# Wider packets for the second weight, renumbered columns of the first layer, and a new order of steps in an RWKV-and-MLP kernel

## The chip, the cores and the metric

The kernel runs on one core of one Trainium2 chip. The metric is the device time of one execution in microseconds (us). A core has five engines that work side by side: TensorE (PE, with its weight loads shown apart as PEld), VectorE (DVE), ScalarE (ACT), GpSimd (POOL) and SyncE (SP). DMAs are issued from SP, ACT and POOL and are moved by sixteen shared DMA engines.

## The reference

Two stages follow each other. The first is a linear attention with decay, for 4 batches, 8 heads, 768 positions and heads of 48:

```python
for t in range(S):
    cur = np.einsum('bhd,bhe->bhde', u[None] * kt, vt)
    y[:, :, t] = np.einsum('bhd,bhde->bhe', rt, state + cur)
    state = w[None, :, :, None] * state + np.einsum('bhd,bhe->bhde', kt, vt)
```

The second is a two-layer network over the 3072 rows of 384 numbers that come out of it, with 2048 columns in the middle:

```python
h = x @ w_in                                   # 384 -> 2048
g = np.where(h >= 1, h, np.where(h <= -1, 0.0, (h + 1) ** 2 / 4))
out = g @ w_out                                # 2048 -> 384
```

## The kernel before

The sequence is cut into twelve groups, g = 0 to 11, of 256 rows each. Groups 0 to 3 are "paired" (256 positions of one batch, two neighbours in a partition); the others hold 128 positions of two batches. Group 0 alone is worked in two halves of its heads for many steps; their names then end in .0 and .1.

Everything is written as named steps, and the string ORDER lists them all: each engine does its steps in the order of that list, in order, and waits where its data isn't there. `@D`, `@A` and `@P` put a step on DVE, ACT or POOL, and `#0` to `#3` name the pair of PSUM banks that the step takes. A pair can be taken again when the tile that held it has been read for the last time. There is no scheduler beside that list.

The steps of one group g, with their engine where it is fixed:

- `ldR`, `ldK`, `ldV` load r, k and v from SP's queue, one load of 384 KB each (half of that for the halves of group 0). Loads of one kind share three buffers (V's are called V32).
- `Rs`, `Ks` multiply r and k with tables of powers of w (W2 for paired groups, made at the start from w by `wB`, `ln`, `wu`, `wd`) into the bf16 tile RK. `Vc` casts v to bf16 (tile Vb).
- `KU` = k times r, `RU` = KU times u, `us` (DVE) = the sum of RU over a head, `ud` = Vb times that sum: the term of the current position, tile V2 or V2b. `uB` and `uc` spread u over all partitions (u_bc).
- `T` (PE) transposes RK, `TT` copies the result to RKT. From group 4 on `RK` does both by a DMA transpose on SP's queue.
- `A` (PE) makes the scores, `AT` (DVE) masks them.
- `Sp` (PE) makes a chunk's part of the state, `Ta`, `Tm` (DVE) and `dc` decay and add it, `sa` and `sb` make bf16 copies for PE.
- `Y` (PE) sums the output of the attention, `y` copies it, adding V2 for unpaired groups. `X` (PE) and `xT` transpose it; from group 4 on `xT` is a DMA transpose on SP's queue.
- `up` g.q (PE) is a quarter of the first layer: 512 of the 2048 columns in four blocks f of 128, 12 matmuls of 256 columns with w_in as the weight that is loaded (line 543). `re` and `sq` (ACT, lines 550 and 554) and `ga` (DVE, line 558) apply the activation.
- `dn` g.j.q (PE) is a quarter of the second layer for 128 of the rows: four matmuls of 384 columns with w_out (line 565). `o` copies the sum (line 123), `st` stores it.

The weights come from POOL's queue, cast to bf16 on the way, each in two halves: `wi` 0 and 1 (line 288) for quarters 0-1 and 2-3 of w_in, `wo` 0 and 1 (line 292) for w_out. Block n of w_out is rows 128 n to 128 n + 127, one row in each partition:

```python
w_out_src = moe_w_out.rearrange("(no ni) d -> ni no d", ni=P)
```

so one partition's share of a block is one piece of 384 numbers, 768 bytes as bf16. `kw` n (line 300) are n matmuls on a tile of zeros whose result nobody reads; they keep PE going in the gaps of the start, in a bank pair that each `kw` names.

Of the kernel before, what the change touches and what calls it, by code (L numbers as in the profile page):

```python
# [9 lines left out]
F32 = mybir.dt.float32  # L10
# [5 lines left out]
P = 128  # L16
# [11 lines left out]
W_IN_ENDS, W_OUT_ENDS = [2, 4], [2, 4]  # L28
# [42 lines left out]


# [1 line left out]
def kernel(  # L74
# [11 lines left out]
    nc = tc.nc  # L86
    B, H, S, D = r.shape
# [4 lines left out]
    nK = DM // P  # L92
    nF = DF // P
    BP = B // 2
    NCH = S // C
    FG = 4
    NQ = nF // FG
# [16 lines left out]
    def bank(slot, what, key, shape, dtype):  # L114
        t = psum.tile(shape, dtype, name=what, tag=f"s{slot}")
        live[(what,) + key] = t
        return t

    def got(what, *key):
        return live[(what,) + key]  # L120
# [8 lines left out]
    w_in_sb = const.tile([P, nK, DF], BF16, name="w_in_sb")  # L129
    w_out_sb = const.tile([P, nF, DO], BF16, name="w_out_sb")  # L130
    w_in_src = moe_w_in.rearrange("(ko ki) n -> ki ko n", ki=P)
    w_out_src = moe_w_out.rearrange("(no ni) d -> ni no d", ni=P)
    mark = const.tile([1, 16], BF16, name="mark")
    w_row = const.tile([1, DM], F32, name="w_row")
    u_row = const.tile([1, DM], F32, name="u_row")
# [152 lines left out]
        nc.gpsimd.dma_start(out=w_in_sb[:, :, n], in_=w_in_src[:, :, n])  # L288

    def step_wo(e, s, i):  # L290
        n = slice(([0] + W_OUT_ENDS)[i] * nF // NQ, W_OUT_ENDS[i] * nF // NQ)
        nc.gpsimd.dma_start(out=w_out_sb[:, n, :], in_=w_out_src[:, n, :])

    def step_mk(e, s, i):
        nc.sync.dma_start(out=mark, in_=w_in_sb[:1, 0, :16])

    def step_kw(e, s, n):
        t = bank(s, "idle", (), [P, 4 * P], F32)
        for _ in range(n):
            nc.tensor.matmul(t, warm[:, :P], warm, start=True, stop=True, skip_group_check=True)  # L300

# [236 lines left out]
    def step_up(e, s, g, q):  # L538
        hp = bank(s, "hp", (g, q), [P, FG, 2 * P], F32)
        for f in range(FG):  # L540
            n0 = (q * FG + f) * P
            for i in range(nK):
                nc.tensor.matmul(  # L543
                    hp[:, f].rearrange("p (j t) -> p j t", j=2), w_in_sb[:, i, n0 : n0 + P], got("xT", g)[:, :, i, :], start=(i == 0), stop=(i == nK - 1),
                    skip_group_check=True,
                )

# [76 lines left out]
```

## Time and profile before

| | |
|---|---|
| three runs, median (lowest to highest) | 179.48 us (179.13 to 179.93) |
| the profiled execution | 179.18 us |
| its span on the core | 177.4 us |
| granted clock of TensorE | 1.00 |
| PE, DVE, ACT, POOL busy | 94%, 72%, 71%, 64% of the span |
| moved by DMA | 28.09 MB, mean 158 GB/s |

The span goes from the first to the last instruction of the program. A row of the order in time gives the start, the length, the engine, the line and the operation, what it writes and reads with the shape, how many were merged (x), and in square brackets how long the engine stood idle before it and what ended that. A row of the waits gives who waited for whom: the total in us, how often, the longest. A row of a DMA queue gives packets, MB and the time of the packets as a share of sixteen engines' time; q1 is SP's queue, q0 POOL's. Durations of PE's matmuls overlap, so the distance from one block to the next is the better measure of what a matmul costs.

### The profile page before, as it was taken

How to read it: one execution, taken by the hardware profiler on the slowest of the kernel's cores; microseconds unless marked ns; L12 is line 12 of the kernel's file. 1: busy time of each engine (PE TensorE's matmuls, PEld its weight loads, DVE VectorE, ACT ScalarE, POOL GpSimd, SP SyncE). 2: the span in 40 equal slices, each digit the busy share in tenths (PEclk: the TensorE clock that was granted, in tenths of full speed). 3: DMA queues.
4: the chain of work that ended last, by engine and by line, in shares of the span. 5: the costliest groups of instructions: out<-in, count | busy, mean ns of one | idle time of the engine just before them, and what ended most of it. 6: DMA issues, size and time to landing. Idle time of an engine off the chain costs nothing.

```text
span 177.4 us, 4658 instructions
## 1 busy us (share of the span) xinstructions
PE 167.6 (94%) x1976; PEld 119.0 (67%) x1979; DVE 127.7 (72%) x152; ACT 125.4 (71%) x151; POOL 113.8 (64%) x95
## 2 busy tenths in 40 slices
PE   7997998979999999999999999999999999899990
PEld 2544677646778678677687766777676875778750
DVE  5789766585577978998737789747879498682660
ACT  2854599866699949639769884489882891777931
POOL 6235959991799999981999453999854593500000
PEclk9999999999999999999999999999999999999999
DMA  6999999999989045919989949989959988140022
GB/s 141 266 256 211 234 221 218 190 221 215 181 209 230 15 93 97 176 40 217 237 134 233 202 82 220 178 159 231 148 143 131 148 188 134 26 137 0 0 89 89
DMA packets 91753, 28.09 MB, mean 158 GB/s; under 512 B 85842, under 2 KB 90964, under 8 KB 91732
## 3 DMA queue, kind: packets, MB, share of 16 engines
q1 hardware_dynamic: 88432, 24.65, 70.8%
q0 software_dynamic: 2880, 3.15, 10.3%
q8 instruction: 15, 0.25, 0.6%
q10 hardware_dynamic: 420, 0.00, 0.1%
q14 instruction: 6, 0.05, 0.1%
HBM read 20.45 MB, written 4.72 MB: 142 GB/s over the span
## 4 chain that ended last, share of the span: by engine, by line
PE 83%; DMA 7%; DVE 4%; ACT 1%; issue 1%; POOL 1%; ACTq 0%; DVEq 0%
PE op L565 35%; PE hp L543 30%; DMA w_out_sb<-in_moe_w_out_dram 7%; PE idle L300 3%; PE A L394 3%; PE Y L508 2%; PE A L388 2%; PE T L359 1%; PE Y L501 1%; PE Sp L426 1%; DVE RK L318 1%; PE Y L480 1%; PE Sp L419 1%; PE X L529 1%; DVE AT L406 1%
## 5 line engine op out<-in xcount | busy, mean ns | idle before, releaser
L558 DVE SCALAR_TENSOR_TENSOR gt<-sq,hp 128x1024 bf16<-128x1024 f32 x48 | 58.1, 1217 | 20.4 <-ACT sq L554 20.1
L565 PE MATMUL op<-w_out_sb,gt 128*128 128x384 bf16 x384 | 70.6, 326 | 2.0 <-DMA w_out_sb<-in_moe_w_out_dram 2.0
L543 PE MATMUL hp<-xT,w_in_sb 128*128 128x256 bf16 x576 | 69.0, 273 | 0.0
L550 ACT ACTIVATE pt<-hp 128x1024 f32<-128x1024 f32 x48 | 48.7, 1017 | 26.0 <-PE hp L543 25.6
L543 PEld LDWEIGHTS <-w_in_sb 128*128 128x128 bf16 x576 | 55.4, 98 | 9.6 <-issue 0.3
L554 ACT ACTIVATE sq<-pt 128x1024 f32<-128x1024 f32 x48 | 50.6, 1057 | 1.4
L565 PEld LDWEIGHTS <-gt 128*128 128x128 bf16 x384 | 35.6, 98 | 22.9 <-issue 1.3
L318 POOL TENSOR_TENSOR RK<-K,W 128x768 bf16<-128x768 f32 (+1 forms) x11 | 19.4, 1764 | 5.7 <-ACT W L267 3.6
L333 POOL TENSOR_TENSOR RU<-KU,u_bc 128x768 f32<-128x768 f32 x11 | 20.0, 1816 | 0.6
L326 POOL TENSOR_TENSOR KU<-K,R 128x768 f32<-128x768 f32 x11 | 20.0, 1820 | 0.0
L318 POOL TENSOR_TENSOR RK<-R,W 128x768 bf16<-128x768 f32 x10 | 18.2, 1825 | 2.5 <-DMA R<-in_r_dram 2.5
L406 DVE TENSOR_TENSOR AT<-A,mask 128x1024 bf16<-128x1024 f32 x16 | 19.1, 1216 | 0.6 <-PE A L394 0.5
L347 POOL TENSOR_TENSOR V<-Vb,us 128x768 f32<-128x768 bf16 x8 | 11.8, 1476 | 8.3 <-ACT Vb L123 5.1
L123 DVE COPY o<-op 128x384 f32<-128x384 f32 x10 | 5.3, 553 | 10.6 <-PE op L565 10.6
L123 ACT COPY o<-op 128x384 f32<-128x384 f32 x14 | 6.2, 479 | 8.0 <-PE op L565 7.9
L339 DVE TENSOR_REDUCE us<-RU 128x16 f32<-128x768 f32 (+1 forms) x13 | 11.4, 882 | 0.0
L460 POOL TENSOR_TENSOR state<-Tm,wCm 128x384 f32<-128x384 f32 (+1 forms) x9 | 7.8, 865 | 5.2 <-DVE Tm L454 4.8
L400 DVE TENSOR_TENSOR AT<-A,mask 128x1024 bf16<-128x1024 f32 x8 | 9.5, 1218 | 2.2 <-PE A L388 2.2
L347 POOL TENSOR_TENSOR V2b<-Vb,us 128x384 bf16<-128x384 bf16 (+1 forms) x4 | 4.6, 1150 | 9.7 <-ACT Vb L123 4.9
L300 PE MATMUL idle<-warm 128*128 128x512 bf16 x22 | 8.4, 493 | 1.6 <-DVE w_col L141 1.2
L523 DVE TENSOR_TENSOR y<-Y,V 128x768 bf16<-128x768 f32 x8 | 7.6, 954 | 0.9 <-POOL V L347 0.3
L123 ACT COPY RKT<-T 128x1024 bf16<-128x1024 bf16 x5 | 5.0, 1013 | 4.4 <-PE T L359 4.4
(85 smaller groups left out, 121.8 us busy)
## 6 DMA issues: line engine op xcount, KB each, us to landing
V<-in_v_dram SPq DMA_DIRECT2D x12, 384.0 KB, 4.8
R<-in_r_dram SPq DMA_DIRECT2D x11, 384.0 KB, 6.2
K<-in_k_dram SPq DMA_DIRECT2D x11, 384.0 KB, 5.7
out_dram<-o SPq DMA_DIRECT2D x7, 384.0 KB, 3.0
out_dram<-o SPq DMA_DIRECT2D x10, 192.0 KB, 3.1
w_in_sb<-in_moe_w_in_dram POOLq DMA_DIRECT2D x2, 768.0 KB, 11.2
w_out_sb<-in_moe_w_out_dram POOLq DMA_DIRECT2D x2, 768.0 KB, 11.0
K<-in_k_dram SPq DMA_DIRECT2D x2, 192.0 KB, 3.1
```

The costliest lines, as they stand in the source:

```text
L123: nc.scalar.copy(out, in_) if e == "A" else engines[e].tensor_copy(out, in_)
L300: nc.tensor.matmul(t, warm[:, :P], warm, start=True, stop=True, skip_group_check=True)
L318: engines[e].tensor_mul(RK[g % NB][:, x, :, hs, :D], rows(got(what, g), g)[:, :, hs], table(x, g, hs))
L326: engines[e].tensor_mul(got("KU", g)[:, :, hs], rows(got("K", g), g)[:, :, hs], rows(got("R", g), g)[:, :, hs])
L333: engines[e].tensor_mul(got("RU", g)[:, :, hs], got("KU", g)[:, :, hs], u_rep)
L347: engines[e].tensor_mul(got("V2", g)[:, :, hs], got("Vb", g)[:, :, hs], sums)
L406: nc.vector.tensor_mul(t.rearrange("p i n t -> p (i n) t"), got("A", g, h).rearrange("p i n t -> p (i n) t"), mask)
L543: nc.tensor.matmul(hp[:, f].rearrange("p (j t) -> p j t", j=2), w_in_sb[:, i, n0 : n0 + P], got("xT", g)[:, :, i, :], start=(i == 0), stop ...
L550: nc.scalar.activation(t, got("hp", g, q), AF.Relu, bias=0.5, scale=0.5)
L554: nc.scalar.activation(t, got("pt", g, q), AF.Square)
L558: nc.vector.scalar_tensor_tensor(out=t, in0=got("sq", g, q), scalar=1.0, in1=got("hp", g, q), op0=ALU.min, op1=ALU.max)
L565: nc.tensor.matmul(got("op", g)[:, j, :DO], got("gt", g, q)[:, f, j * P : (j + 1) * P], w_out_sb[:, n, :], start=(n == 0), stop=(n == nF - 1),
```

## The change

Four things change, and with them some line numbers by one.

The rows of w_out are dealt out anew: of the 512 rows of a quarter q, partition p takes the four neighbours 4p to 4p + 3. They lie side by side in memory, so a partition's share of a quarter is one piece of 4 x 384 numbers, 3072 bytes as bf16. For the second layer to meet the right rows, block f of the first layer's quarter must hold the columns 4p + f. The weight tile w_in stays as it is in memory; the matmul of `up` reads every fourth column of it, a step of 8 bytes.

The idle matmuls take one bank pair once (`kw5#0`) and later ones write to the same tile (`got("idle")`), where each block took a pair of its own before. There are 18 instead of 25.

All steps stand in a new order. Some change their engine: KU0.0, RU0.1, dc1, ud1, Vc7, Vc9 and sb4 go to POOL; KU1, TT1.0, TT3.0, uc, wu1.1, y3 and o1.0, o2.1, o3.1 to DVE; Vc5, Vc8, sa0, sb0, sb7, xT0, o2.0 and the o copies of groups 4, 6, 8 and 9 to ACT.

```diff
 ORDER = """
-wr@A ur@A kw6#0 wB0#0 ldK0.0 ldR0.0 ldR0.1 cl tb KU0.0@D ln0 wu0.0@A wu1.0@D wd1.0@A wd0.0@D Rs0.0@D Ks0.0@D ldK0.1
+wr@A ldK0.0 ur@A cl ldR0.0 ldK0.1 ldR0.1 tb kw5#0 wB0#1 ln0 wd1.0@A wd0.0@D wu0.0@A wu1.0@D Rs0.0@D wB1#2 ln1 wd1.1@A
...
-    w_out_src = moe_w_out.rearrange("(no ni) d -> ni no d", ni=P)
+    w_out_src = moe_w_out.rearrange("(q p f) d -> p q (f d)", p=P, f=FG)
...
     def step_wo(e, s, i):
-        n = slice(([0] + W_OUT_ENDS)[i] * nF // NQ, W_OUT_ENDS[i] * nF // NQ)
-        nc.gpsimd.dma_start(out=w_out_sb[:, n, :], in_=w_out_src[:, n, :])
+        q = slice(([0] + W_OUT_ENDS)[i], W_OUT_ENDS[i])
+        nc.gpsimd.dma_start(out=w_out_sb.rearrange("p (q f) d -> p q (f d)", f=FG)[:, q, :], in_=w_out_src[:, q, :])
...
     def step_kw(e, s, n):
-        t = bank(s, "idle", (), [P, 4 * P], F32)
+        t = got("idle") if s is None else bank(s, "idle", (), [P, 4 * P], F32)
...
     def step_up(e, s, g, q):
...
-            n0 = (q * FG + f) * P
             for i in range(nK):
                 nc.tensor.matmul(
-                    hp[:, f].rearrange("p (j t) -> p j t", j=2), w_in_sb[:, i, n0 : n0 + P], got("xT", g)[:, :, i, :], ...
+                    hp[:, f].rearrange("p (j t) -> p j t", j=2), w_in_sb.rearrange("p i (q n f) -> p i q f n", q=NQ, f=FG)[:, i, q, f], got("xT", g)[:, :, i, :], ...
```

75 lines of the change are left out of this document (37 added, 38 removed).

## Prediction

> **What bounds the kernel now.** I read the waits first, then the engines' busy time by stretch, then the order in time of the first 42 us on each engine.
>
> ```profile
> PE op L565 <- DMA w_out_sb<-in_moe_w_out_dram: 2.0, 2, 1.2
> PE Y L501 <- DVE AT L406: 0.5, 1, 0.5
> ...
> 41.00:61.00 20.00, 20.00 (x342) 14.91 (x335) 13.81 (x18) 16.94 (x25) 15.13 (x11) 1.00 0.92 178
> 121.00:141.00 20.00, 20.00 (x214) 14.48 (x213) 15.12 (x15) 14.78 (x17) 12.78 (x9) 1.00 0.94 164
> ```
>
> In the two rows by stretch the columns are the length, then the busy time of PE, PEld, DVE, ACT and POOL, the granted clock, the DMA share and GB/s. PE has no gap there: 20.00 of 20.00 at clock 1.00, and no other engine is near its limit. So between about 41 and 173 us only PE's own work counts, and it is the same matmuls in both kernels. Time can be won only where PE is not yet full, or does work that nobody needs: the start, the two waits for w_out, and the half microsecond at the last Y.
>
> ```profile
> 1.19 2.74 PE L300 MATMUL idle<-warm 128*128 128x512 bf16 x6 [1.19 <-DVE w_col L141]
> ...
> 10.79 0.62 PE L359 MATMUL T<-ident,RK 128*128 128x128 bf16 x8
> ...
> 19.49 0.50 PE L529 MATMUL X<-ident,y 128*128 128x128 bf16 x6
> ...
> 20.85 2.79 PE L543 MATMUL hp<-xT,w_in_sb 128*128 128x256 bf16 x24
> ...
> 26.48 4.09 PE L543 MATMUL hp<-xT,w_in_sb 128*128 128x256 bf16 x36
> 31.39 2.77 PE L565 MATMUL op<-w_out_sb,gt 128*128 128x384 bf16 x16 [0.82 <-DMA w_out_sb<-in_moe_w_out_dram]
> ...
> 37.08 1.46 PE L565 MATMUL op<-w_out_sb,gt 128*128 128x384 bf16 x8 [1.16 <-DMA w_out_sb<-in_moe_w_out_dram]
> ```
>
> The first row of the first layer (up0.0) starts at 20.85; from there to 30.57 PE is dense. It then stands 0.82 us for the first half of w_out, and 1.16 us for the second. What sets 20.85 is DVE, which works through this without a long gap:
>
> ```profile
> 6.50 0.55 DVE L318 TENSOR_TENSOR RK<-R,W 128x384 bf16<-128x384 f32 x1
> 6.97 0.55 DVE L318 TENSOR_TENSOR RK<-K,W 128x384 bf16<-128x384 f32 x1
> ...
> 9.19 0.68 DVE L123 COPY RKT<-T 128x1024 bf16<-128x1024 bf16 x1
> ...
> 11.83 0.95 DVE L318 TENSOR_TENSOR RK<-R,W 128x768 bf16<-128x768 f32 x1
> 12.69 0.95 DVE L318 TENSOR_TENSOR RK<-K,W 128x768 bf16<-128x768 f32 x1
> 13.56 1.02 DVE L333 TENSOR_TENSOR RU<-KU,u_bc 128x384 f32<-128x384 f32 x2
> 14.50 1.00 DVE L339 TENSOR_REDUCE us<-RU 128x8 f32<-128x384 f32 x2
> 15.42 0.35 DVE L436 TENSOR_TENSOR state<-Sp,wCm 128x192 f32<-128x192 f32 x1
> 15.80 0.36 DVE L451 TENSOR_TENSOR Tm<-Sp,state 128x192 f32<-128x192 f32 x1
> 16.07 3.48 DVE L400 TENSOR_TENSOR AT<-A,mask 128x1024 bf16<-128x1024 f32 x3
> ```
>
> **The start.** The first block of idle matmuls loses one of six, 2.74 / 6 = 0.46 us, so the broadcast of w and all behind it can begin 0.46 us earlier if the row of w has landed by 3.5 us; the trace does not show that landing, and if it is late this term is 0. On DVE I add up the new order from Rs0.0 (now at 6.50 - 0.46 = 6.04) to AT0.1, from start to start in the rows above: three operations of half a tile 3 x 0.47, wu1.1 0.35 (nearest row: 15.42), the copy u_bc 0.46 (below, on ACT), TT0.0 0.68, RU0.0 0.47, us0.0 0.46, Rs0.1 0.47, Rs1 0.86, Ta0 0.38, us0.1 0.46, AT0.0 1.16, Tm0 0.27, AT0.1 1.16. That is 8.6 us, so AT0.1 ends at 14.6. Before it ended at 16.07 + 1.16 = 17.2: the gain is that Ks1, one RU and one KU go behind it or to POOL. Waits: Rs1 is reached at 10.3, and it needs the load of R1.
>
> ```profile
> 3.44 0.80 SPq L227 DMA_DIRECT2D R<-in_r_dram  x1
> ...
> R<-in_r_dram SPq DMA_DIRECT2D x1, 384.0 KB, 5.7
> ...
> q1 hardware_dynamic: 4818, 1.81, 112.2%
> ...
> L123 ACT COPY u_bc<-uB 128x384 f32<-128x384 f32 x1 | 0.5, 455 | 0.0
> ...
> L123 ACT CAST y<-Y 128x768 bf16<-128x768 f32 x3 | 2.4, 789 | 0.4 <-PE Y L487 0.4
> ```
>
> R1 landed at 3.44 + 5.7 = 9.1. V1 now goes ahead of it on SP, and SP's queue moved 1.81 MB from 2 to 9 us, so 0.39 MB more is 1.5 us: R1 lands at 10.6, a wait of 0.3. I put AT0.1's end at 15.0.
>
> From there to up0.0 took 20.85 - 17.2 = 3.6 us. Now two branches run. One is Y0.1, y0.1, X0 (0.50) and xT0, which is a copy on ACT (0.8 by the y row): some 2.9 us with Y0.1's 0.7. The other decides, since PE takes A1.0 and T1.1 ahead of up0.0: Ks1 0.86, KU1 0.86, TT1.0 0.68 on DVE, then A1.0 (sixteen small matmuls, at most the 0.51 of the L508 row below) and T1.1 (0.62) on PE, 3.5 us. So up0.0 starts at 18.5, at 19.0 if w lands late: 2.4 or 1.9 earlier. A1.1, some 0.4 us, was ahead of up0.0 and is now behind it: **net 1.5 to 2.0, I take 1.8**. The six up blocks from there to the first dn0 are the same and took 9.7 us; ACT has the same work in that stretch, so I cost its new order at nothing.
>
> In these rows the names are tiles: RK the scaled r and k, KU and RU the products for the diagonal, AT the masked scores, W2 the tables. DVE before, from the first RK:
>
> ```order
> L318 TENSOR_TENSOR RK_78<-R_148,W2_133 128x2x4x48
> L318 TENSOR_TENSOR RK_78<-K_146,W2_134 128x2x4x48
> L326 TENSOR_TENSOR KU_154<-K_146,R_148 128x2x192
> L318 TENSOR_TENSOR RK_78<-R_148,W2_133 128x2x4x48
> L123 COPY RKT_189<-T_180 128x1024
> L400 TENSOR_TENSOR AT_213<-A_196,mask2_109 128x1024
> L318 TENSOR_TENSOR RK_79<-R_218,W2_133 128x16x48
> L318 TENSOR_TENSOR RK_79<-K_220,W2_134 128x16x48
> L333 TENSOR_TENSOR RU_294<-KU_154,u_bc_71 128x2x192 x2
> ```
>
> And DVE now, from the copy of the first transposes to the second AT:
>
> ```order
> L122 COPY RKT_189<-T_180 128x1024
> L334 TENSOR_TENSOR RU_191<-KU_166,u_bc_71 128x2x192
> L340 TENSOR_REDUCE us_194<-RU_191 128x2x4
> L319 TENSOR_TENSOR RK_78<-R_141,W2_133 128x2x4x48
> L319 TENSOR_TENSOR RK_79<-R_202,W2_133 128x16x48
> L437 TENSOR_TENSOR state_122<-Sp_206,wCm_84 128x192
> L340 TENSOR_REDUCE us_194<-RU_191 128x2x4
> L401 TENSOR_TENSOR AT_262<-A_245,mask2_109 128x1024
> L452 TENSOR_TENSOR Tm_329<-Sp_206,state_122 128x192
> L401 TENSOR_TENSOR AT_335<-A_286,mask2_109 128x1024
> ```
>
> The full RK from K_220 (Ks1) no longer stands between the two AT, and one of the two RU is gone from DVE.
>
> **The weight loads.** POOL issues them, and each row here gives start and length of the issue; the rows of landings are of w_in, then of w_out.
>
> ```profile
> 8.79 1.71 POOL L288 DMA_DIRECT2D w_in_sb<-in_moe_w_in_dram  x2
> ...
> 19.48 1.81 POOL L333 TENSOR_TENSOR RU<-KU,u_bc 128x768 f32<-128x768 f32 x1
> 21.24 0.94 POOL L292 DMA_DIRECT2D w_out_sb<-in_moe_w_out_dram  x1
> ...
> 25.23 0.94 POOL L292 DMA_DIRECT2D w_out_sb<-in_moe_w_out_dram  x1
> ...
> DMA to landing us min/median/max: 9.7/11.2/12.7
> ...
> DMA to landing us min/median/max: 10.1/11.0/11.8
> ...
> q0 software_dynamic: 269, 0.52, 91.3%
> q1 hardware_dynamic: 268, 0.10, 19.4%
> ...
> q0 software_dynamic: 381, 0.29, 92.9%
> q1 hardware_dynamic: 383, 0.08, 34.2%
> ...
> q1 hardware_dynamic: 1778, 0.35, 123.7%
> ```
>
> POOL before, from its first scaled k to the first half of w_out (state and sd are the running state, V2b the diagonal term):
>
> ```order
> L318 TENSOR_TENSOR RK_78<-K_146,W2_134 128x2x4x48
> L288 DMA w_in_sb_66<-in_moe_w_in_dram 128x3x1024 x2
> L347 TENSOR_TENSOR V2b_301<-Vb_224,us_298 128x2x192
> L123 CAST sd_126<-state_122 48x4x48 x2
> L347 TENSOR_TENSOR V2b_301<-Vb_224,us_298 128x2x192
> L326 TENSOR_TENSOR KU_402<-K_220,R_218 128x768
> L333 TENSOR_TENSOR RU_430<-KU_402,u_bc_71 128x768
> L292 DMA w_out_sb_67<-in_moe_w_out_dram 128x8x384
> ```
>
> POOL now, over the same stretch:
>
> ```order
> L327 TENSOR_TENSOR KU_166<-K_136,R_141 128x2x192
> L319 TENSOR_TENSOR RK_78<-K_136,W2_134 128x2x4x48
> L289 DMA w_in_sb_66<-in_moe_w_in_dram 128x3x1024
> L334 TENSOR_TENSOR RU_191<-KU_166,u_bc_71 128x2x192
> L348 TENSOR_TENSOR V2b_243<-Vb_198,us_194 128x2x192 x2
> L289 DMA w_in_sb_66<-in_moe_w_in_dram 128x3x1024
> L461 TENSOR_TENSOR state_122<-Tm_329,wCm_84 128x192
> L334 TENSOR_TENSOR RU_453<-KU_384,u_bc_71 128x768
> L293 DMA w_out_sb_67<-in_moe_w_out_dram 128x2x1536
> ```
>
> The second half of w_in was issued right behind the first; it now stands behind two V2b, which wait for us0.1 on DVE. By the sum above us0.1 ends at 12.4, so that issue starts at 13.2 instead of 9.7. Alone in its queue it lands 9.7 us later, at 22.9; up0.2, its first user, is reached two up blocks (1.31 each), A1.1 and Y1 (about 1.0) after up0.0, 4.0 us, at 22.5 to 23.0. A wait of 0 to 0.4: **minus 0.3**. The first half goes out 0.46 us earlier than before and lands by 18.0, half a microsecond ahead of up0.0.
>
> The first half of w_out stands behind RU1, which needs KU1 (DVE, 15.0 + 0.86 + 0.86 = 16.7): 16.7 + 1.8 = 18.5 instead of 21.24. The second stands behind a V2b and two state steps that need us1 and Tm1, by the same sums at about 22.7 instead of 25.23. The packets: the last pairs of rows are the packets, MB and engine time of POOL's queue q0 and SP's q1 from 15 to 18 us (w_in, 2048 bytes) and from 33 to 35 us (w_out, 768 bytes). Both times the queues take turns packet by packet, 269 to 268 and 381 to 383. A turn takes 16 x 3 / 269 = 178 ns with 2048 bytes and 16 x 2 / 381 = 84 ns with 768; a line through both gives 250 ns with 3072. A half of w_out is 1024 packets before, 64 for each of 16 engines, 5.4 us; now 256, 16 for each, 4.0 us. So a half lands 1.4 us sooner after its issue: 18.5 + 10.1 - 1.4 = 27.2 and at most 22.7 + 11.8 - 1.4 = 33.1. PE reaches the first dn0 at 30.57 - 1.8 + 0.3 = 29.1, and the first matmul of the second half four dn blocks (2.6), one up and one T later, at 33.5. **Both waits go: 0.82 + 1.16 = 2.0.** If the packets changed nothing, the second half would land at 34.5 and 1.0 us would stay.
>
> The Trainium skill, "DMA: Bandwidth & Descriptors", Specifications, says that 512 bytes are enough for line rate. By that sentence alone 768-byte packets lose nothing, and that 1.0 us would stay.
>
> **The strided weights.** 576 weight loads now read every fourth column. The trace has no strided load; the bounds come from these rows:
>
> ```profile
> L543 PEld LDWEIGHTS <-w_in_sb 128*128 128x128 bf16 x576 | 55.4, 98 | 9.6 <-issue 0.3
> ...
> 104.59 1.31 PE hp L543 x12
> ...
> 113.37 0.51 PE Y L508 x16
> ```
>
> A pair of load and matmul takes 1.31 / 12 = 109 ns here, and 0.51 / 16 = 32 ns where the matmul is short (L508, same size of load). So a load needs at most 32 of the 109 ns and may become 3.4 times slower before PE feels it. Below, 0; above, at a quarter of the speed, 4 x 32 - 109 = 19 ns x 576 = 10.9 us. I take 0, since the L508 row is the same load.
>
> The Trainium skill, "SBUF — State Buffer", in its note on SBUF "cachelines", has lines of 16 bytes and full bandwidth with two or more accesses in a line. A step of 8 bytes has just two, so by that note it is free, at the limit; no row here shows it.
>
> **The rest.** At the last Y the wait of 0.47 (the 0.5 row) came from an o copy between the two AT of the last group on DVE; it is on ACT now: **0.5**. Eight o copies go to ACT, four V casts swap between ACT and POOL; both engines have slack in the rows by stretch, so nothing. The 18 idle matmuls left fill gaps. A new order may open gaps of its own: SP's loads run at their limit up to 42 us, and now PE wants them 4 us earlier. I take **minus 0.5** for Sp3 and T3.0, with 0 and 5 as ends (below).
>
> Sum: 1.8 - 0.3 + 2.0 + 0.5 - 0.5 = 3.5 us. The profiled execution took 179.18 us (span 177.4 and 1.8 around it), 0.3 under the median of 179.48, inside the runs' spread. 179.2 - 3.5 = **175.7 us**.
>
> **Rivals.** *SP's loads starve.* As the queues take turns by packet, fewer and larger packets of q0 mean fewer turns for q1. Before there was a pause of q0 between w_in and w_out, in which q1 moved 1778 packets from 23 to 25 us (the last row). Now w_out's first half is issued before w_in is through. If the three later halves follow each other without a pause, q1 gets only 384 + 256 + 256 turns in them, less than one load of 1024 packets: K2 lands when w_out is through, near 33, Ks2 follows on POOL at 34.8 where T2.0 is reached at 32.4, and the products of the next two groups come late by up to 3 more: 5.5 us in place of the 0.5 above, 175.2 + 5.5 = 180.7. It turns slower where these waits pass 4.0. For it: the turn counts. Against it: the four issues stand near 8.3, 13.2, 18.5 and 22.7, 4.2 to 5.3 us apart, and a half takes 24 x 178 ns = 4.3 us (w_in) or 4.0 (w_out), which leaves q1 pauses. Chance 0.20, most of it with a smaller price, 177 to 180.5.
>
> *Strided loads slow PE.* At a quarter of the speed 179.2 - 3.5 + 10.9 = 186.6; it decides against the change from 115 ns a pair, 6 ns over now. Against it stands the reserve in the L508 row. Chance 0.09.
>
> *Packets change nothing.* 1.0 us stays: 176.7. The two turn lengths speak against it. Chance 0.08.
>
> *Stalls later in the new order*, at xT8 or xT10, whose transposes by DMA follow y more closely: 178 to 181. PE's and DVE's sums leave about half a microsecond there. Chance 0.05.
>
> **How the numbers follow.** Forecast 0.58, from 173.9 to 177.0: the largest terms (2.4 at the start, no wait for w_in, no new wait) give 174.3, the smallest (1.5, 0.4, and 1.0 of new waits) 176.6, and 0.4 on either side is the spread of the runs. Of the starvation, 0.07 is still over 0.5% faster, 0.08 within, 0.05 slower; strided loads 0.09 slower; packets 0.08 faster; later stalls 0.02 within, 0.03 slower. Faster by over 0.5% (0.9 us, about what a measurement of this kernel can tell): 0.73, same 0.10, slower 0.17. The range 173.9 to 181.0 leaves out the strided case, the worst of the starvation and a little below.
>
> **What would show it.** Right: up0.0 near 18.5, no wait of L565 for w_out, pairs of L543 still at 109 ns, PE 20.00 of 20.00 in the middle. Wrong: L543 blocks of 12 over 1.38 us; PE waits for T or Sp between 30 and 50 us with POOL waiting for R or K; up0.2 waiting for w_in.

## The result, and the profile after

| | before | after |
|---|---|---|
| median (lowest to highest) | 179.34 us (179.13 to 179.93) | 187.24 us (185.84 to 187.84) |
| the profiled execution | 179.18 us | 187.2 us |
| its span | 177.4 us | 185.4 us |
| granted clock of TensorE, mean | 1.00 | 0.978 |
| ratio to before, 95% interval | | 1.0424 [1.036, 1.0487] |

The change makes the kernel 4.2% slower, where 175.7 us was forecast with a range up to 181.0. The two profiled executions differ by 8.0 us, and the places are few. Where the highest execution of a kernel below stands 3 us or more above its others (e2, e6, e10), it is left out of the ratio. The first row is the top of the page: busy time, share and instructions of each engine, with the granted clock by fortieths of the span. Then come the waits of PE and of the copies on ACT, from the view of the waits, and last the copies' row of before.

```profile
PE 171.0 (92%) x1970; PEld 126.3 (68%) x1972; DVE 127.3 (69%) x148; ACT 125.9 (68%) x155; POOL 115.0 (62%) x95
PEclk9999957999999999999999999999999999999998
```

```profile
ACT o L122 <- PE op L565: 27.8, 10, 4.7
...
PE hp L543 <- DMA w_in_sb<-in_moe_w_in_dram: 4.0, 1, 4.0
...
PE op L565 <- DVE gt L558: 2.3, 3, 1.5
```

```profile
ACT o L123 <- PE op L565: 7.9, 5, 3.1
```

The two waits of L565 for w_out that stood in the profile of before are gone. In their place are a wait of 4.0 us for w_in, which before did not have, and 2.3 us in which PE waits for the activated values. The clock falls in the sixth and seventh fortieth, and a little in the last. The rows by stretch give length, busy time of PE, PEld, DVE, ACT and POOL, clock, DMA share and GB/s:

```profile
21.00:31.00 10.00, 6.23 (x75) 4.31 (x75) 3.91 (x5) 3.33 (x4) 8.62 (x9) 0.66 1.12 216
31.00:41.00 10.00, 10.00 (x102) 8.74 (x95) 5.35 (x5) 9.87 (x11) 8.75 (x5) 1.00 0.95 200
...
61.00:81.00 20.00, 19.56 (x208) 14.04 (x206) 15.62 (x17) 13.37 (x15) 19.06 (x13) 1.00 0.63 112
81.00:101.00 20.00, 19.56 (x241) 15.49 (x240) 15.35 (x17) 13.83 (x17) 14.17 (x11) 1.00 0.92 160
101.00:121.00 20.00, 18.50 (x177) 14.09 (x176) 12.46 (x12) 14.37 (x17) 14.37 (x8) 1.00 0.90 194
...
141.00:161.00 20.00, 19.42 (x202) 13.93 (x200) 14.74 (x14) 13.03 (x17) 13.48 (x9) 1.00 0.78 158
```

PE stands for 3.8 us of the stretch from 21 to 31. The mean clock there is 0.66; from 24 to 30 us, when PE works again, it is 0.50. In the middle, where before had no gap but the half microsecond at the last Y, it stands 0.44 + 0.44 + 1.50 + 0.58 = 3.0 us. PE in order of time at the first place:

```profile
20.45 0.27 PE L543 MATMUL hp<-xT,w_in_sb 128*128 128x256 bf16 x1
24.77 2.54 PE L543 MATMUL hp<-xT,w_in_sb 128*128 128x256 bf16 x11 [4.05 <-DMA w_in_sb<-in_moe_w_in_dram]
27.24 0.64 PE L389 MATMUL A<-RKT 48*64 48x128 bf16 x16
27.81 2.68 PE L543 MATMUL hp<-xT,w_in_sb 128*128 128x256 bf16 x12
```

up0.0 does one matmul, at 20.45, and then stands for 4.05 us until the second half of w_in is in. It needs only the first half. The rest of it and up0.1 take some 2.5 us each, where a block of twelve takes 1.31 elsewhere: two cold blocks, 2.4 us, the price of the clock.

The second place is in the middle. First PE, then ACT, in the same stretch of the order in time:

```profile
68.13 1.47 PE L543 MATMUL hp<-xT,w_in_sb 128*128 128x256 bf16 x12
...
69.90 0.82 PE L565 MATMUL op<-w_out_sb,gt 128*128 128x384 bf16 x4
...
74.57 0.82 PE L565 MATMUL op<-w_out_sb,gt 128*128 128x384 bf16 x4 [0.40 <-DVE gt L558]
```

```profile
65.29 0.82 ACT L122 CAST Vb<-V 128x768 bf16<-128x768 f32 x1
70.76 0.48 ACT L122 COPY o<-op 128x384 f32<-128x384 f32 x1 [4.66 <-PE op L565]
71.14 1.03 ACT L550 ACTIVATE pt<-hp 128x1024 f32<-128x1024 f32 x1
72.20 1.06 ACT L554 ACTIVATE sq<-pt 128x1024 f32<-128x1024 f32 x1
```

PE has up3.0 ready at 69.6. ACT could take it, but it stands 4.66 us in front of the copy o2.0, whose sum PE finishes only at 70.7, and begins re3.0 at 71.14. re3.0, sq3.0 and ga3.0 are what dn3.0.0 waits for, and it starts 0.40 us late. The same pattern stands at o3.0 ahead of re4.0, at o5.0 ahead of re6.1 (PE's longest gap there, 1.50), and at o8.1 behind sq9.1, where A10.1 waits for the bank. The o5.0 place, ACT first and then PE:

```profile
111.39 0.48 ACT L122 COPY o<-op 128x384 f32<-128x384 f32 x1 [2.39 <-PE op L565]
...
115.46 0.82 PE L565 MATMUL op<-w_out_sb,gt 128*128 128x384 bf16 x4 [1.50 <-DVE gt L558]
```

Of these four copies only o2.0 and o8.1 are new on ACT. o3.0 and o5.0 were on ACT before as well; there the new order alone put the copy ahead of an activation that could run.

Two theories come out of this. **F**, the false wait: the matmul that now reads every fourth column of the one tile w_in is made to wait for both halves of it, and the 4 us of idling then cost the clock. **Q**, the copies: o copies that stand in ACT's queue ahead of the activation hold that up. The rivals: that reading with a step slows every block, that the 3072-byte packets took turns from w_in or SP, and that the second half of w_in was simply issued too late.

The wait as it stands in the program, the first layer's loads and matmuls with their waits, from the instruction list of after:

```
L543 LDWEIGHTS w_in_sb [waits DMASW0_49]
L543 MATMUL hp<-xT,w_in_sb 128x256 [waits Activation_49]
L543 LDWEIGHTS w_in_sb [waits DMASW1_49]
```

DMASW0 is the first half's DMA, DMASW1 the second's. In the list of before the wait for DMASW1 stands at the first load of up0.2, 64 loads behind the first one of up0.0.

The first load doesn't wait for the second half, the second load does. In a partition w_in is 3 rows of 2048 elements, and the second half's DMA writes the last 1024 of each, so it spans 1024 to 6143. The first load reads from 0 to 508, ahead of that span; the second reads from 2048 to 2556, inside the span, where the DMA writes nothing. In before the second load reads 2048 to 2175 in the same gap and doesn't wait. This fits a rule that compares a view with a step by its span and one of neighbours by its elements; no run tried it by itself.

### The profile page after: what moved, and what is told of

The parts are those of the page before. It is cut to its first block, busy times and chain, and to the rows that moved or that the text cites. A ratio compares the mean times of both kernels' runs of the same rounds, so it can differ in the third digit from the quotient of the medians.

```text
span 185.4 us, 4639 instructions
## 1 busy us (share of the span) xinstructions
PE 171.0 (92%) x1970; PEld 126.3 (68%) x1972; DVE 127.3 (69%) x148; ACT 125.9 (68%) x155; POOL 115.0 (62%) x95
## 3 DMA queue, kind: packets, MB, share of 16 engines
HBM read 20.45 MB, written 4.72 MB: 136 GB/s over the span
## 4 chain that ended last, share of the span: by engine, by line
PE 77%; DMA 8%; DVE 5%; ACT 5%; issue 2%; SPq 1%; POOL 0%; ACTq 0%; DVEq 0%
PE op L565 34%; PE hp L543 32%; DMA w_in_sb<-in_moe_w_in_dram 5%; PE A L395 3%; DMA R<-in_r_dram 2%; ACT sq L554 2%; DVE gt L558 2%; ACT pt L550 2%; PE Y L509 2%; PE T L360 1%; DVE RK L319 1%; PE Sp L427 1%; PE A L389 1%; PE Y L502 1%; PE Y L481 1%
## 5 line engine op out<-in xcount | busy, mean ns | idle before, releaser
L543 PE MATMUL hp<-xT,w_in_sb 128*128 128x256 bf16 x576 | 72.0, 279 | 4.1 <-DMA w_in_sb<-in_moe_w_in_dram 4.0
L565 PE MATMUL op<-w_out_sb,gt 128*128 128x384 bf16 x384 | 70.5, 327 | 2.3 <-DVE gt L558 2.3
L543 PEld LDWEIGHTS <-w_in_sb 128*128 128x128 bf16 x576 | 62.9, 115 | 9.5 <-DMA w_in_sb<-in_moe_w_in_dram 4.3
L565 PEld LDWEIGHTS <-gt 128*128 128x128 bf16 x384 | 35.2, 98 | 23.8 <-DVE gt L558 3.2
L122 ACT COPY o<-op 128x384 f32<-128x384 f32 x19 | 8.5, 481 | 28.0 <-PE op L565 27.8
L334 POOL TENSOR_TENSOR RU<-KU,u_bc 128x768 f32<-128x768 f32 (+1 forms) x12 | 21.0, 1751 | 3.3 <-DVE KU L327 2.1
L327 POOL TENSOR_TENSOR KU<-K,R 128x768 f32<-128x768 f32 (+1 forms) x11 | 19.2, 1750 | 3.9 <-DMA R<-in_r_dram 3.9
L461 POOL TENSOR_TENSOR state<-Tm,wCm 128x384 f32<-128x384 f32 (+1 forms) x10 | 8.4, 840 | 10.5 <-DVE Tm L455 7.3
L348 POOL TENSOR_TENSOR V<-Vb,us 128x768 f32<-128x768 bf16 x8 | 11.8, 1480 | 3.0 <-DVE us L340 2.8
L348 POOL TENSOR_TENSOR V2b<-Vb,us 128x768 bf16<-128x768 bf16 (+1 forms) x5 | 6.3, 1253 | 11.0 <-ACT Vb L122 7.0
L301 PE MATMUL idle<-warm 128*128 128x512 bf16 x16 | 7.5, 582 | 1.7 <-DVE w_col L142 1.2
L360 PE MATMUL T<-ident,RK 128*128 128x128 bf16 x64 | 5.9, 242 | 1.2 <-DVE RK L319 1.2
L360 PEld LDWEIGHTS <-RK 128*128 128x128 bf16 x64 | 4.7, 108 | 3.4 <-DVE RK L319 2.7
```

What stands on the lines that cost most here:

```text
L327: engines[e].tensor_mul(got("KU", g)[:, :, hs], rows(got("K", g), g)[:, :, hs], rows(got("R", g), g)[:, :, hs])
L334: engines[e].tensor_mul(got("RU", g)[:, :, hs], got("KU", g)[:, :, hs], u_rep)
L348: engines[e].tensor_mul(got("V2", g)[:, :, hs], got("Vb", g)[:, :, hs], sums)
L360: nc.tensor.transpose(t[:, i, :], RK[g % NB][:, x, j, 2 * p : 2 * p + 2, :].rearrange("p h d -> p (h d)"), ident)
L543: nc.tensor.matmul(hp[:, f].rearrange("p (j t) -> p j t", j=2), w_in_sb.rearrange("p i (q n f) -> p i q f n", q=NQ, f=FG)[:, i, q, f], got ...
L565: nc.tensor.matmul(got("op", g)[:, j, :DO], got("gt", g, q)[:, f, j * P : (j + 1) * P], w_out_sb[:, n, :], start=(n == 0), stop=(n == nF - 1),
```

## The experiments

Each run has before beside it on the same chip: 179.21 us for e1 to e4, 179.51 for e5 to e8, 179.71 for e9 to e11. The ratios are against those, and where two kernels of different groups are compared, the difference is taken from the ratios (0.01 is 1.8 us). Line numbers differ from run to run; what a row writes and reads (hp from w_in_sb, op from w_out_sb) tells the step.

**e1_split.** The weight w_in as two tiles, one for each half, so that the first half's reads cannot touch the second half's write. Order and packets stay.

```diff
-    w_in_sb = const.tile([P, nK, DF], BF16, name="w_in_sb")
+    w_in_sb = [const.tile([P, nK, DF // 2], BF16, name="w_in_sb", tag=f"wi{i}") for i in range(2)]
...
-        nc.gpsimd.dma_start(out=w_in_sb[:, :, n], in_=w_in_src[:, :, n])
+        nc.gpsimd.dma_start(out=w_in_sb[i], in_=w_in_src[:, :, n])
```

> The changed kernel with w_in kept in two tiles, one for each half, and nothing else altered. Theory F (false wait): the strided reading of one tile makes the second weight load of up0.0 wait for the second half of w_in, which it doesn't read. Then here up0.0 runs on from about 20.5 us with no wait, the clock stays at 1.00 from 21 to 31 us, and 4.05 us of waiting and about 2.4 us of half speed go: 187.2 - 6.4 = 181 us. Rival D (the data itself is late, because DMA is saturated): up0.0 still stands until 24.8 and the time stays at 187. Rival S (strided loads are slow): the time stays within 1 us of 187.

Measured: 180.97 us (180.71 to 182.24), ratio 1.0112 [1.0067, 1.0156], clock 1.00. PE in order of time:

```profile
20.05 1.47 PE L543 MATMUL hp<-xT,w_in_sb 128*128 128x256 bf16 x12
21.45 0.42 PE L389 MATMUL A<-RKT 48*64 48x128 bf16 x16
21.80 1.50 PE L543 MATMUL hp<-xT,w_in_sb 128*128 128x256 bf16 x12
...
25.28 1.50 PE L543 MATMUL hp<-xT,w_in_sb 128*128 128x256 bf16 x12 [1.01 <-DMA w_in_sb<-in_moe_w_in_dram]
...
30.88 2.76 PE L565 MATMUL op<-w_out_sb,gt 128*128 128x384 bf16 x16
```

The wait is now where the data are used first, at up0.2, and 1.01 long. The first block of the second layer starts at 30.88; in after it stands at 36.99. The medians differ by 6.3 us, the ratios by 5.6, and F's share is shown. The kernel is still 1.1% slower than before, so F is not all. The half was issued too late as well: 1.01 us of waiting is left with no false wait.

**e2_wi1_early.** One tile again, but the second half of w_in issued right behind the first.

```diff
-... wu1.1@D wi0 wc uB#3 ... ud0.1@P Vc1@A wi1 kw2 T0.1#1
+... wu1.1@D wi0 wi1 wc uB#3 ... ud0.1@P Vc1@A kw2 T0.1#1
```

> The changed kernel with the second half of w_in issued right behind the first (near 8.6 us instead of 15.0), one tile. Theory F: the false wait is still there, but the half lands near 20.5 to 21.5 (12.7 us after its issue, as before the change), so at most 1 us of it is left and the clock stays up: 181 to 182 us. Rival D: as the queues share the engines the half lands later than 23 and R2 and K2 are late too: 184 to 187. Rival S: 186 to 187.

Measured: 181.69 us (181.01 to 185.13), ratio 1.0125 [1.008, 1.017]. PE in order of time, then the clock from 21 to 31:

```profile
21.49 1.39 PE L508 MATMUL hp<-xT,w_in_sb 128*128 128x256 bf16 x11 [1.11 <-DMA w_in_sb<-in_moe_w_in_dram]
```

```profile
21.00:31.00 10.00, 9.51 (x132) 8.91 (x133) 6.47 (x7) 8.40 (x10) 9.15 (x9) 1.00 1.15 231
```

The false wait is still at the second matmul, but short, 1.11 us, because the half lands earlier. With it the clock stays at 1.00. Strided reading and packets are those of after, and 5.4 to 5.5 us are back, so neither can be the cause of them. So the late issue and the false wait are two factors of one cost: taking either away gives most of it back.

**e3_layout** and **e4_layout_split.** The order of before with the new packets and columns; e3 has w_in in one tile, e4 in two.

```diff
-    w_out_src = moe_w_out.rearrange("(no ni) d -> ni no d", ni=P)
+    w_out_src = moe_w_out.rearrange("(q p f) d -> p q (f d)", p=P, f=FG)
...
-                    ... w_in_sb[:, i, n0 : n0 + P], ...
+                    ... w_in_sb.rearrange("p i (q n f) -> p i q f n", q=NQ, f=FG)[:, i, q, f], ...
```

> The kernel before, its order of steps untouched, with the packets of 3072 bytes and the strided columns alone, one tile for w_in. Theory F: up0.0's second load waits from 21.0 until the second half of w_in lands at 22.4, 1.5 us, and the two waits for w_out, 2.0 us, go or nearly go: 178.5 to 179.5 us. Rival S: 576 slower loads, 186 or more. If the packets bring nothing: 180.5 to 181.

> As the run before (order of steps of the kernel before, wider packets, strided columns), with w_in in two tiles. Theory F with useful packets: no wait at up0.0, no wait for w_out: 179.3 - 2.0 = 177.3 us. Packets without use: 179.3. Rival S: 186 or more, with blocks of twelve L543 pairs over 1.38 us instead of 1.31.

Measured: e3 178.94 us (178.46 to 180.91), ratio 0.9999 [0.9966, 1.0031]; e4 177.66 us (176.82 to 178.09), ratio 0.9907 [0.9873, 0.9942]. The only wait of the first layer for w_in in e3's profiled execution:

```profile
23.39 4.36 PE L544 MATMUL hp<-xT,w_in_sb 128*128 128x256 bf16 x23 [2.47 <-DMA w_in_sb<-in_moe_w_in_dram]
```

The false wait comes with the layout, whatever the order: 2.47 us in e3, where the half is issued early. It eats up what the packets bring. In e4 neither weight is waited for, and the layout is worth 0.93%, 1.7 us. Its blocks are no slower for it. The matmuls and weight loads of the first layer in e4, from the groups (busy time, mean ns of one, idle time before):

```profile
L544 PE MATMUL hp<-xT,w_in_sb 128*128 128x256 bf16 x576 | 69.2, 273 | 0.1
...
L544 PEld LDWEIGHTS <-w_in_sb 128*128 128x128 bf16 x576 | 62.2, 114 | 3.9 <-DMA xT<-y 0.5
```

A load is recorded at 114 ns instead of the 98 of before, and the blocks of twelve still come every 1.31 us.

**e5_o_moved** and **e6_o_moved_wi1.** e1 with the copies that stood in the way moved: o2.0, o3.0, o8.0 and o8.1 on DVE, o5.0 behind sq6.1. e6 has the early issue of e2 as well.

```diff
-... dc5@P o2.0@A o2.1@D re3.0 ... dn3.1.3 o3.0@A o3.1@D re4.0 ... dn5.1.3 o5.0@A Rs8@P ... sq6.1 ga6.1 ... o8.0@A sq9.1 o8.1@A
+... dc5@P o2.0@D o2.1@D re3.0 ... dn3.1.3 o3.0@D o3.1@D re4.0 ... dn5.1.3 Rs8@P ... sq6.1 o5.0@A ga6.1 ... o8.0@D sq9.1 o8.1@D
```

> The run with w_in in two tiles, with five copies of the second layer's sums taken out of ACT's way: o2.0, o3.0, o8.0 and o8.1 on DVE (o2.0 and o8 as before the change), o5.0 on ACT but behind sq6.1. Theory Q (a copy that waits for PE at the head of ACT's queue holds up re, sq and ga behind it): PE's four waits of 0.40, 0.40, 1.50 and 0.58 us and the slower restart after each (about 0.15) go: 181.0 - 3.4 = 177.6 us. Rival T (ACT or DVE simply has too much work there): the waits move to other steps and the time stays within 1 us of 181.

> As the run before, and the second half of w_in issued right behind the first. Theory F and Q: the wait of 1.0 us at up0.2 goes too: 176.6 us, the fastest of all if the earlier start (up0.0 at 20.05 instead of 20.85) keeps what it is worth. Rival D (the loads of R2 and K2 come late instead, as the queues share the engines): 177.5 to 178.5.

Measured: e5 177.5 us (177.11 to 177.69), ratio 0.9893 [0.9868, 0.9919]; e6 177.13 us (176.56 to 184.5), ratio 0.9865 [0.9824, 0.9905]. A row of the waits and three stretches of e5:

```profile
ACT o L87 <- PE op L530: 15.5, 6, 4.1
```

```profile
61.00:81.00 20.00, 20.00 (x234) 16.21 (x233) 16.88 (x19) 13.67 (x15) 19.91 (x14) 1.00 0.74 143
101.00:121.00 20.00, 20.00 (x240) 15.21 (x239) 14.91 (x15) 16.73 (x20) 14.59 (x11) 1.00 0.86 162
141.00:161.00 20.00, 20.00 (x214) 15.23 (x213) 13.94 (x13) 14.14 (x16) 3.78 (x3) 1.00 0.36 85
```

PE has no gap any more in the stretches that had them. Against e1 the moved copies are worth 3.5 us by the medians and 3.9 by the ratios, and Q is shown for the five copies together; they were not moved one by one. ACT still waits 15.5 us for sums, but at places that PE doesn't feel. In e6 the early issue brings 0.4 us, within the intervals, of the 0.92 that e5 still waits for w_in: K1 and R1 come later there, and the transposes wait 1.9 us for scaled r and k.

**e7_clock.** After, with sixteen idle matmuls ahead of up0.0. They write to the bank that up0.0 takes next, and their result is not read.

```diff
     def step_up(e, s, g, q):
         hp = bank(s, "hp", (g, q), [P, FG, 2 * P], F32)
+        for _ in range(16 if (g, q) == (0, 0) else 0):
+            nc.tensor.matmul(hp[:, :2].rearrange("p f t -> p (f t)"), warm[:, :P], warm, ...)
```

> The changed kernel, its false wait left in, with 16 idle matmuls in front of up0.0 (into the bank that it overwrites), so that PE works through most of the wait. They take 16 x 0.216 = 3.5 us, so up0.0 still ends its wait near 24.8. Theory C (the wait itself is only 4.05 us of the loss; the idle time lets the clock fall, and that costs 2.4 more): granted clock 1.00 from 21 to 31 us, and 187.2 - 2.4 = 184.8 us. If the clock's fall costs nothing: 187.2.

Measured: 184.75 us (184.43 to 184.89), ratio 1.0294 [1.0264, 1.0323].

```profile
20.21 3.62 PE L542 MATMUL hp<-warm 128*128 128x512 bf16 x16
23.66 0.27 PE L545 MATMUL hp<-xT,w_in_sb 128*128 128x256 bf16 x1
25.03 1.39 PE L545 MATMUL hp<-xT,w_in_sb 128*128 128x256 bf16 x11 [1.10 <-DMA w_in_sb<-in_moe_w_in_dram]
26.36 0.42 PE L389 MATMUL A<-RKT 48*64 48x128 bf16 x16
26.71 1.50 PE L545 MATMUL hp<-xT,w_in_sb 128*128 128x256 bf16 x12
```

The second matmul starts at 25.03, a little later than in after, yet the kernel is 2.5 us faster by the medians and 2.3 by the ratios and by the spans: eleven matmuls take 1.39 us instead of 2.54. Its clock from 21 to 31 us is 1.00, in the row below, where after has 0.66. That is the price of the clock by itself.

```profile
21.00:31.00 10.00, 8.90 (x115) 6.55 (x113) 3.69 (x6) 5.03 (x6) 8.86 (x8) 1.00 1.12 215
```

The Trainium skill, "TensorE: Matmul & The Clock Gate", Part 1, says that the clock halves after an idle window of about 3.4 us and that the window runs freely. The runs agree in part: 0.66 over ten microseconds after 4.05 us idle, 1.00 after the 1.01 of e1 and the 1.11 of e2; but in e3's profiled execution it fell after 2.47 us too.

**e8_step16.** e4 with blocks of eight columns, so that a partition's piece of w_out is 6144 bytes and the matmul reads every eighth column, a step of 16 bytes.

```diff
-    w_out_src = moe_w_out.rearrange("(q p f) d -> p q (f d)", p=P, f=FG)
+    w_out_src = moe_w_out.rearrange("(h p f) d -> p h (f d)", p=P, f=2 * FG)
...
-                    ... w_in_sb[q // 2].rearrange("p i (q n f) -> p i q f n", q=NQ // 2, f=FG)[:, i, q % 2, f], ...
+                    ... w_in_sb[q // 2].rearrange("p i (n f) -> p i f n", f=2 * FG)[:, i, q % 2 * FG + f], ...
```

> The order of steps of the kernel before with two tiles of w_in, and the renumbering doubled: block f of eight holds the columns 8p + f of half the layer, a step of 16 bytes, and w_out comes in packets of 6144 bytes. Against the same with a step of 8 bytes (177.66 us). Theory M (a load needs at most 32 of the 109 ns, so a step of 16 bytes stays hidden although the recorded load grows past 115 ns): blocks of twelve pairs stay at 1.31 us, 177 to 178. Rival L (one access in a line of 16 bytes instead of two halves the rate and it shows): blocks over 1.38 us and 3 to 15 us more.

Measured: 178.32 us (177.64 to 179.0), ratio 0.9938 [0.9917, 0.9959].

```profile
L543 PEld LDWEIGHTS <-w_in_sb 128*128 128x128 bf16 x576 | 64.4, 145 | 3.2 <-DMA xT<-y 0.6
```

The recorded load is 145 ns now, half as long again as with neighbouring columns, and the blocks of twelve still come every 1.31 us. So the loads of these blocks have a reserve at 16 bytes too, and at 8 the strided reading costs nothing. The packets of 6144 bytes land sooner again, 7.6 to 8.3 us after the issue, where those of 3072 take 9.6 in e4 and those of 768 take 10.1 to 11.8 in before. They bring no time: no wait for w_out was left to take.

**e9_order_alone.** e5's order with the layout of before: 768-byte packets, neighbouring columns, one tile.

```diff
-    w_out_src = moe_w_out.rearrange("(q p f) d -> p q (f d)", p=P, f=FG)
+    w_out_src = moe_w_out.rearrange("(no ni) d -> ni no d", ni=P)
...
-                    ... w_in_sb[q // 2].rearrange(...)[:, i, q % 2, f], ...
+                    ... w_in_sb[:, i, (q * FG + f) * P : (q * FG + f + 1) * P], ...
```

> The changed order of steps with the five o copies moved (as in the run of 177.5 us), but w_out in packets of 768 bytes and contiguous columns, one tile of w_in, as before the change. What the packets are worth in the new order: with landings 10.1 and 11.8 us after the issue, w_out's halves come near 30.3 and 36.4, where PE is there at 30.5 and 34.9: a wait of about 1.5 us, 179.0 us. If packets bring nothing: 177.5. The contiguous loads should be recorded at 98 ns again and the blocks stay at 1.31 us.

Measured: 179.25 us (177.98 to 180.26), ratio 0.9986 [0.9951, 1.0021].

```profile
30.93 2.77 PE L530 MATMUL op<-w_out_sb,gt 128*128 128x384 bf16 x16 [0.40 <-DMA w_out_sb<-in_moe_w_out_dram]
...
36.54 1.46 PE L530 MATMUL op<-w_out_sb,gt 128*128 128x384 bf16 x8 [1.08 <-DMA w_out_sb<-in_moe_w_out_dram]
```

Both waits for w_out are back, and with them 0.93%, 1.7 us. One tile read in neighbouring columns does not wait falsely: the wait for w_in stands at up0.2 (0.76). The new order alone, with its copies mended, is as fast as the old one.

**e10_wi1_mid** and **e11_before_o9.** The best of each order: e5 with wi1 issued ahead of the two V2b, and e4 with o9.0 moved behind AT11.1.

```diff
-... RU0.1@P us0.0 ldV0 ... Vc1@A wi1 kw2 T0.1#1
+... RU0.1@P wi1 us0.0 ldV0 ... Vc1@A kw2 T0.1#1
```

```diff
-... us11 o9.0@D AT11.1 o9.1@D st9
+... us11 AT11.1 o9.0@D o9.1@D st9
```

> The run of 177.5 us with the second half of w_in issued ahead of the two V2b instead of behind them, near 10.5 us instead of 14.9. It should land near 21 to 22, before up0.2 at 24, without taking turns from R1 and K1: the wait of 0.92 us goes and 176.6 us is left. If the turns it takes make R1 or K1 late, T1.0 waits and it stays at 177 to 177.5.

> The order of steps of the kernel before with the wider packets, strided columns and two tiles of w_in (177.66 us), and o9.0 on DVE moved behind AT11.1. The last Y's wait of 0.47 us goes: 177.2 us. If the copy only pushes the wait elsewhere: 177.7.

Measured: e10 176.57 us (176.55 to 182.08), ratio 0.9827 [0.9774, 0.9881], with no wait for either weight; e11 177.0 us (176.76 to 177.23), ratio 0.9851 [0.9796, 0.9906], with one of 0.39 for w_out. These two beat both kernels. Their intervals overlap, so whether the new order is worth anything beyond the old one stays open.

## Why the prediction was wrong, step by step

**The weight loads, w_in: the step that failed.** "up0.2, its first user" is true of the data and not of the program. The minus 0.3 became 4.05 of waiting and 2.4 of clock, together 6.4; e1 gives 5.6 to 6.3 back, 0.4 of it because its up0.0 starts at 20.05 and not at 20.45, and keeps 1.01 of waiting. The trace of before could not show it. The list of instructions could: the wait for the second half had moved from the first load of up0.2 to the second load of up0.0. I used the order for what stands where and not for what each instruction waits on. That the strided view of one tile ties loads of the first half to the DMA of the second is shown by the pairs after and e1, e3 and e4, and by e9, where the contiguous view waits at the right place. Among the signs of being wrong the prediction had up0.2 waiting for w_in; what waited was up0.0, for a half that it doesn't read. The times of the step were off as well: us0.1 ended on DVE at 14.2 instead of 12.4, so the issue came at 15.01 instead of 13.2, and the half was in at 24.73, so that even two tiles wait 1.01 where I allowed 0.4.

**"Eight o copies go to ACT ... so nothing": the second failure.** I asked whether ACT has slack over a stretch of 20 us, and it has. But it works in order, and a copy whose sum isn't ready takes the slack of what is queued behind it. The waits of copies on ACT went from 7.9 us in five places to 27.8 in ten, and four places reached PE. The eight copies that moved account for two of them, o2.0 (0.40) and o8.1 (0.58). The other two, o3.0 (0.40) and o5.0 (1.50), are copies that were on ACT already, so the larger part belongs to "a new order may open gaps of its own", for which 0.5 was set aside at Sp3 and T3.0. The price of all together is 3.5 to 3.9 us (e5 against e1); how it falls on the single copies was not measured.

**The start.** Forecast 1.8 net, got nothing: up0.0 at 20.45 instead of 20.85, and A1.1 behind it takes the 0.4 back. The order of the steps was right, and the sum from AT0.1 to up0.0 too (3.75 for 3.5); AT0.1 itself ended at 16.7 instead of 15.0. Three rows of DVE of after, three of POOL, then one of each of before:

```profile
6.88 1.30 DVE L327 TENSOR_TENSOR KU<-K,R 128x384 f32<-128x384 f32 x1 [0.26 <-DMA R<-in_r_dram]
...
10.17 0.71 DVE L334 TENSOR_TENSOR RU<-KU,u_bc 128x384 f32<-128x384 f32 x1
...
11.38 2.05 DVE L319 TENSOR_TENSOR RK<-R,W 128x384 bf16<-128x384 f32 x2
```

```profile
6.77 1.00 POOL L319 TENSOR_TENSOR RK<-K,W 128x384 bf16<-128x384 f32 x1 [0.92 <-ACT W L268]
...
9.47 0.99 POOL L334 TENSOR_TENSOR RU<-KU,u_bc 128x384 f32<-128x384 f32 x1 [0.83 <-DVE u_bc L122]
...
11.61 1.01 POOL L348 TENSOR_TENSOR V2b<-Vb,us 128x384 bf16<-128x384 bf16 x1 [1.15 <-DVE us L340]
```

```profile
7.97 1.30 DVE L318 TENSOR_TENSOR RK<-R,W 128x384 bf16<-128x384 f32 x1
```

```profile
7.67 1.18 POOL L318 TENSOR_TENSOR RK<-K,W 128x384 bf16<-128x384 f32 x1 [3.65 <-ACT W L267]
```

Beside a product on POOL, DVE's products of half a tile took 1.30 instead of 0.55, in before as well, in a row that I left out. I priced them all at 0.47. KU0.1 lost 0.75 so, beside Ks0.1 on POOL, and the pair Rs0.1 and Rs1 0.65 (1.98 from start to start, for 0.47 + 0.86), beside a V2b. Those two steps were on POOL before as well; the new order puts other steps of DVE beside them. Of the two that the change moved to POOL, RU0.1 cost RU0.0 0.27 (0.74 from start to start), and KU0.0 stood beside none of these products. The three losses make 1.7 us, which is what AT0.1 is late by. The Trainium skill, "SBUF — State Buffer", section "SBUF: two separate sides", says that an operation of VectorE with two inputs from SBUF and a GpSimd operation that reads SBUF exclude each other for a whole instruction. These rows agree: KU0.1 and RU0.0 each end 0.4 us after POOL's product, and so does the row of before. No experiment tried it apart. (The lower end of the range took 2.4 for the start, where the term's own net was 2.0 at most; the outcome is not touched by it.)

**w_out: right.** No wait for it in after, e1 to e8 and e10. A half landed 8.7 to 9.1 us after its issue in after. In one and the same order it landed after 9.6 instead of 10.1 to 11.8 us (e4 against before) and after 9.4 to 10.3 instead of 10.7 to 12.5 (e5 against e9), so sooner by about 0.5 to 2.2 us where the turns gave 1.4. The turns themselves were not so regular in after: from 20 to 22 us POOL's queue moved 200 packets and SP's 41. The layout is worth 1.7 us in the new order (e5 against e9) and in the old (e4 against before); 2.0 was forecast. The Trainium skill ("DMA: Bandwidth & Descriptors", Specifications) has 512 bytes as enough for line rate. By that alone 768 bytes would lose nothing; here, beside SP's queue, the layout with them was 1.7 us slower.

**Strided loads: right.** The reserve of the L508 row (Y, in before) covers them, at 8 bytes (after, e4) and at 16 (e8). That the strided rival's 186.6 is near the result is an accident: the pace is 109 ns a pair wherever the clock is 1.00. By the Trainium skill, "SBUF — State Buffer", note on "cachelines", full bandwidth needs two accesses in a line of 16 bytes, and a step of 16 bytes has one; the recorded load is longer (145 ns), though it is at 8 bytes too (114), and in the pace neither shows.

**The rest.** The half microsecond at the last Y went. The rival of SP's loads did not come to PE: no wait of PE for a T or an Sp between 30 and 50 us. Nor did PE wait at xT8 or xT10, where the rival of later stalls had put them.

In sum, from the terms as measured: start 0, w_in -6.4, w_out +1.7, last Y +0.5, copies -3.5 to -3.9, which is 7.7 to 8.1 us slower; the profiled executions differ by 8.0.

The case of slower was left to strided loads, starved queues and stalls at xT8 or xT10, and none of them happened. No rival had an instruction waiting for data that it doesn't read, and none had ACT standing in front of an input.

## What to carry to other kernels

When a change alters how a tile is indexed, compare which instruction waits for which DMA before and after, and not only the order of the instructions: a view with a step can tie a reader to a write that it does not touch, and a tile for each separately loaded part removes that. A copy moved to an in-order engine with slack is free only if its input is ready when the engine gets there; look at what is queued behind it. A long wait on TensorE is to be priced with the clock that it may lose, here 2.4 us on top of 4.05.

## What the runs showed of the hardware that I had not expected

Reading weights with a step lengthens the recorded load, from 98 ns for neighbouring columns to 114 at a step of 8 bytes and 145 at 16, and the pace of 109 ns a pair of load and matmul stays the same. At 16 bytes 576 loads of 145 ns make 83.5 us where PEld is busy for 64.4: the records overlap, so a load's recorded length is no measure of what PE can bear.

The clock can fall after less idling than in after. In e3's profiled execution, after 2.47 us:

```profile
24.00:26.00 2.00, 2.00 (x12) 1.42 (x10) 0.00 (x0) 0.04 (x1) 1.91 (x5) 0.50 1.24 209
```

That execution took 180.91 us, the longest of e3's, whose median is 178.94. So a wait of this length seems to lose the clock in some executions and not in others; that was not tried by itself. In e8's profiled execution the clock fell at the start, where PE's waits were shorter still, at most 0.7 us between 6 and 16 us:

```profile
6.00:11.00 5.00, 3.79 (x64) 2.04 (x64) 4.18 (x7) 3.83 (x10) 2.85 (x3) 0.67 1.25 266
11.00:16.00 5.00, 4.89 (x43) 2.58 (x41) 4.97 (x10) 1.30 (x3) 1.09 (x2) 0.65 1.12 212
```

That execution took 178.98 us, where e8's median is 178.32. Why the clock fell there is not shown.
